# A two-layer attention and token-MLP kernel: weight loads in 256 KB pieces, and new order tables

## The chip, the cores and the metric

The kernel runs on one core of a Trainium2 chip. The metric is the time of one execution on the device in microseconds (us). The engines are TensorE (PE in the profile, with its weight loads as PEld), VectorE (DVE), ScalarE (ACT), GpSimd (POOL) and SyncE (SP), which here issues nearly all DMAs.

## The reference, cut to what matters

The input is x of 2048 tokens by 512 features, in bfloat16. Two blocks alternate, each twice, and both add their result to x.

```python
def _A_ref(x, wqkv, wo):                     # sliding-window attention, 32 heads of 16, window 256
    qkv = (x @ wqkv).reshape(B, S, 3, H, Dh) ...
    scores = einsum("bhqd,bhkd->bhqk", q, k) * Dh ** -0.5
    mask = (i - j >= 0) & (i - j < W)
    o = einsum("bhqk,bhkd->bhqd", softmax(where(mask, scores, -1e9)), v)
    return o... @ wo

def _B_ref(x, w1, b1, w2, b2):               # MLP over tokens
    u = gelu(einsum("bsd,sf->bdf", layernorm(x), w1) + b1)     # 2048 -> 1792
    return (einsum("bdf,fs->bds", u, w2) + b2).transpose(0, 2, 1)

x = x + _A_ref(layernorm(x), wqkv, wo);  x = x + _B_ref(layernorm(x), w1, b1, w2, b2)
x = x + _A_ref(layernorm(x), wqkv, wo);  x = x + _B_ref(layernorm(x), w1, b1, w2, b2)
```

## The kernel before

x stays on the chip as 16 tiles of 128 tokens (`x_sb`). A layer is one attention and one token MLP; there are two.

**Attention.** Queries go in four blocks (Q) of 512 tokens. For each block the normalised x is transposed into `xhT` (the first block by PE, L517, and copied out by DVE or ACT, L518; the others by DMA transposes issued from SP, L507), and `project` (L528) multiplies it by `wqkv`. K and Q are copied out of PSUM through a mask (`masked`, L544); V is copied (L599), transposed by DVE (L601) and spread into `v_sb` (L593). The heads form four groups t. For each block and group nine steps m follow: `emit_scores` (L689) writes two PSUM banks with quarter-array matmuls, ACT takes their exponential (`emit_exp`, L695), DVE or POOL multiply the edges of the window by a triangle (L713), and `emit_pv` (L739) multiplies by V into two other banks, 4 and 5. Two pairs of banks alternate for the scores, so the scores of step m + 2 wait for the exp of step m.

After the ninth step the two value banks are copied out, one into `oU` (L743) and one into `o2` (L744), by DVE or ACT, and only then may the next group write them. After every second group three small DMAs (`den_c`, L754) gather the softmax denominators and one of 256 KB (L755) moves half of `o2` into `oU`. `o2` has room for two groups, so a later copy into it waits for these DMAs. `job_inverse` and `job_normalise` then divide, and `job_outproj` (L656) multiplies by `wo` and adds to x, followed by the statistics of the next layernorm (`ln_stats`, bn_stats at L460).

**Token MLP.** `w1` has seven blocks fb of 256 columns, each in four quarters q of 512 tokens (256 KB). Blocks 0 to 2 have a home of their own, `w1buf`; block 3 takes over `xhT`, blocks 4 and 5 `k_sb`, block 6 `q_sb`, as soon as these are free (`w1_place`). `w1_half_dma` (L831) loads half a block of `w1buf`, 512 KB, `w1_dma` (L827) a quarter of the others. `u_product` (L862) and `job_u` make the products, `job_y` (L935) the second matrix with `w2` loads of 512 and 384 KB (`w2_dma`) into `w1buf` and `oU`. Parts of the first matrix product (`job_u_part`) and of the second are put between the attention's steps, so that PE has other work while ACT does exps.

**Order.** Every job makes operations (`Plan.op`) with the buffers they read and write, in a fixed numbering. Which engine does each one, and in what order each engine does its own, stands in the tables `ORDER`, written as two letters of `ALPHABET` per operation; `BANKS` gives the PSUM bank, 6 or 7, of each short-lived result. `arrange` reads them, and `needs` derives the semaphore waits. An engine goes through its own list strictly in order, SP with its DMAs included: what stands behind a waiting DMA issue waits too. SP's DMAs take 16 semaphores in turn, so that an issue also waits for the landing of the sixteenth before it.

**Beginning.** PE first does groups of ten small warm-up matmuls (L449), ten such groups in all, most of them before any result is needed. The loads come first on SP: x tiles 0, 1 and 2 to 3, the halves of the K and Q weights, x tiles 4 to 7, the V weights (into the home of w1's block 2, from where `turn_weights`, L437, reorders them). `first_half` (L564) makes the first K and Q group in two halves of 256 tokens each, so that the second half needs only the last two transposes.

Of the kernel before, what the change touches and what calls it, by code (L numbers as in the profile page):

```python
# [33 lines left out]
O0OmOsO6NqPBOzO5PFM0PKPAPSQYPZPEPfPJPPPVPjPtNkPNPYPyPeP4PcPiPsQAQHPoPxP3P-QRO3QGQVQKQbP7QoQfQkRXQvQUQaQeQ1Q-Q5QjQuRDORRKQ0Q4ROQsRUQ+RHRcQERhRNRTRbRmRg
RlRzR0RRSuR3R4R5SvSrSsS3S0S4SxSGS1S2SDS6S5SRSJSySVS7SNSwStSoSlSzSpSmSqTHSnTDTFTBTZS9S8S-TaThTNTVTOTiTRTSTWTdTeTLTJT0UFT5UGT1T6UAUBUqUUUvUZUjUfUrUdUbUk
VQU8UVUhUoUwVAVEVSVIWjWkVMVWVbYeVpVkYfVhVuV1VaX5X6VyV6VjVoV+VtV0V5WGWTWoV9WNWFWVWDW4WfWaWKXYXGWRWwWrXHWZW1WeW9WqWvW0XCZoW8XBXNXUXdXrYzXiXnZeYCXwXcX1Xh
XmXvX0X-YXYMYHaNZ3YTYaX+aOYuYGYLYQY1a+Y6YZY-Yta-ZEZIYyY5Y+ZDZPalZZZHZOZSZhboZrZlZMbpZyZgZ5cLZ+ZkZqZxaCbHaKZ1aVaHZ9aiaBaJaSaeaYayadarahbEaqaaaxa6a5bDbS
cObNbldZbMbhcPbybRb2babVb6cjcDbkbtb1cIb5aucbcCcHcgdrcocNcfcsa1c0clc4eVdAcrczdEbudRc3c-dDdQdVdUdcb9ehdmdbduc7dzdfeFd5eAcvdteHdyd4d-eMgIeQeDeYeueeeLeneP
eXeberd2ezfLe7emfDejeqfIeye6fCfQe2fVfHfPfUfcfjfrfnfvgrfmfzfqfyf3gff-f2gFe+gLf+gEgQiLgYgKgPgcgVh8gkgogTgbgwgjgngvg0fYhBgzhFf6hQhkhbhAhfiohEhmhMhKhqhxhU
h0h1h4heh-hjhNhpiDhwh3iIiaiQh+iCiXiHiNiehOiiibisixiWiTidihi3iriwi2i-ili+jGjKjHjRjYkZjVjUjbjojfi6jkjajejwkAj2jjj6jskEjvj1kLjtkPj5j-kWjDkIkejEkjkOkVkdko  # L40
kiknk1k2kSkTk5k6k7lwl8l5lzl2l9l6lIltlulFl3lxlXlPl0lLlTlylvl1l4lqlrlsl7mHmJmBmPmjmDmQmFlnmTmkmblomXmfmgmUmcmYl+lpl-mLmNmzm9m+mvnDnEm5m6mwnHnIm0nNnbnjnf
# [5 lines left out]
NzMYMXMvL5MmL6MHNRM8MzMnNhL7NVNWNbMIMTN3NiNjMUMoOPOMO-N9OgN-MVOZOoPnOrOCOwOxNrM1O9QZOBPWPXPRM2PbPOPhPdP6PpPqQJO4QLQMQXP8P9QdQCQDQTRYQpQqQrQhRAQ3QyOSRB
QtP+RIRJRZRCRoRpRaRsRqRSR6R7RxQFRvSASCSHSISFSESSSKSWSXSTSOSLSPSMSQSUSYSZSbSfSgTbTPTjTTTXTfUHT7UKT2T+T3UCT-ULUDT4UEUOUMUaUTUgUeUcUsU9UlU+UmUiUnUWUxUtVC
VFUyVGUXWlUuUzUYVNU0VLVYVOU2VeVVYgYjVmVnU4ViV3VxVrX7V4WmVzWAWUWpWJV8WEW5WnWXWMW6W7X8XaWPWYYkX9WcWQXIW3XLXbZpXMYlXWXPY0XEXtXXXlXFZfXpXyYDYYX3YnYBYsYqXq
YpZ4YPYEYSYVYRY3YxaPY4Y8Y9bAZBZKZUbBanZTZNbqZuZtbCZncMZ7ZvbrZ8aAaFaIaUaXaTaZatacbJa0bGaba8aQdacQbncRbUb0aRbsbccSbWckbXcTawcGavcVcddscicqbYcucncma2cXc6  # L50
# [10 lines left out]
AJAKASATAMAiALANBCAOAPBGCJCCB-CKAmApCLArAsCMCNCOCPBiAqB3BkB9BnBlBmCqClC0CmCrC5DGDACIDMC6DHCQDZDQDRCRCSDgFpCHDhDaDuDoAkD6FrEEEMCEFsCTFtENCBCUEcFuEdEwCV
ExErE6CWFQB+FXFLCXFeFYFMFRFfF6F7F-GEGAGKGFCYHpGVGfGrGnCZIFIGJOG-HEHAHIG0CDHXJQJTJRCFHtIUIBCGJSIKIPILIiIuCAI8JBJUI3I9JkJcKDKFKJKNCbKvKrKHLDLELIKGLNLUK4
LoL3MMMEMAMjNANGM7NPNHNZNpNfN7N8NvOIOVN+OAONCaOkODO2OvOEO8PHPDOyPUPIPMPvPlP0P1QmM3QxQ7RFQ8RMRQRWReRjR2RrRtSaScUNUPURTuUSU-VDVUVKU1U3VdTsU7VZU6VwU5TqVs
WITpWBWhWiWtWyWdWzWuYmXfW-XAXkXgXzTrX4YoYOYJXuYcYwYKYdYWTtZCZGZjaoZLapZRZbZ0aEZwaMakagbLbPa9bjbQb4b8cFbZcUcKcec2cWdGcYcacBdodwdYdecAeJeKeOeCepd+eaeget
# [6 lines left out]
BANKS = (
    "76766776777676767667766666677676777767776666667677677767666776666776676767677677667767766777666767676776776666677766676776776676677676676676"
    "766677666777777667666776777676766767776666776776766776677766")


class Res:
# [990 lines left out]
```

## Time and profile before

| | us |
|---|---|
| median of three runs (489.77 to 489.91) | 489.77 |
| the profiled execution, whole | 490.92 |
| its span, first to last instruction | 489.2 |
| PE busy | 480.0 (98%) |
| DVE busy | 335.3 (69%) |
| ACT busy | 319.7 (65%) |
| POOL busy | 199.6 (41%) |
| PE, PEld clock granted | 1.00 in every window |

The span contains everything from the first to the last instruction on any engine; the whole execution adds the start and end of the program. "Busy" counts time in which at least one instruction of the engine ran, so PE can be busy and yet lose a little where a group starts late behind another that still drains. L numbers are lines of the kernel. In a row of the timeline the text in brackets is the idle time of the engine before that instruction and what ended it. The first attention lies between 12 and 161 us of the span, its MLP up to about 235, the second attention up to 395, and the last MLP to the end.

### The profile page before, as it was taken

Reading aid. Unit: us, or ns where it says so; the run is one execution under the profiler, and the core shown is the slowest. Engines: PE = TensorE matmul, PEld = TensorE weight load, DVE = VectorE, ACT = ScalarE, POOL = GpSimd, SP = SyncE. Lnnn points to the kernel's source line nnn. Section 1 sums busy time; section 2 is a strip of 40 time slices with the busy share of each in tenths; the row PEclk is TensorE's granted clock in tenths of the full one; section 3 lists DMA queues with packets and bytes.
Section 4 is the critical chain, followed back from the end, with each engine's and each line's share of the span. In section 5 each row is a group of like instructions: output and inputs, shape, how many; then the busy total and the mean of one; then the engine's idle time right before and its main releaser. Section 6 shows DMA issues by size and latency. Waiting matters only on the chain.

```text
span 489.2 us, 17263 instructions
## 1 busy us (share of the span) xinstructions
PE 480.0 (98%) x7706; PEld 255.4 (52%) x7706; DVE 335.3 (69%) x707; ACT 319.7 (65%) x391; POOL 199.6 (41%) x365
## 2 busy tenths in 40 slices
PE   7999998999999999999999999999999999999997
PEld 6544555555556444444445555556556544444444
DVE  7999998889988550246798777999977646122123
ACT  4999998999989313302767889999999940240000
POOL 5988884534726100022624544465644721000000
PEclk9999999999999999999999999999999999999999
DMA  6442024400228780350024300130222957030842
GB/s 194 92 119 56 27 60 100 70 5 27 27 58 223 215 228 1 107 147 5 1 44 132 89 27 3 37 62 6 68 70 77 261 148 204 0 98 10 228 150 86
DMA packets 83722, 43.59 MB, mean 89 GB/s; under 512 B 19008, under 2 KB 82624, under 8 KB 83648
## 3 DMA queue, kind: packets, MB, share of 16 engines
q1 hardware_dynamic: 79776, 42.48, 32.1%
q0 software_dynamic: 3872, 0.02, 1.2%
q8 instruction: 60, 0.98, 0.8%
q14 instruction: 14, 0.11, 0.1%
HBM read 32.51 MB, written 2.10 MB: 71 GB/s over the span
## 4 chain that ended last, share of the span: by engine, by line
PE 91%; ACT 5%; DMA 1%; DVE 1%; SPq 1%; issue 0%
PE ps L859 20%; PE ps L932 19%; PE ps L526 17%; PE ps L684 14%; PE ps L733 12%; PE ps L653 6%; ACT p_sb L695 4%; PE ps L777 1%; DMA x_sb<-in_A_x_dram 1%; PE ps L919 1%; SPq L352 1%; PE ps L446 0%; DVE o L358 0%; DVE q_sb L537 0%; ACT vT L360 0%
## 5 line engine op out<-in xcount | busy, mean ns | idle before, releaser
L695 ACT ACTIVATE p_sb<-ps 128x1024 bf16<-128x1024 f32 (+8 forms) x288 | 261.1, 974 | 23.5 <-PE ps L684 18.5
L712 POOL TENSOR_TENSOR p_sb<-p_sb,edge 128x256 bf16<-128x256 bf16 (+2 forms) x223 | 106.8, 494 | 102.7 <-ACT p_sb L695 88.0
L684 PE MATMUL ps<-q_sb,k_sb 64*64 64x288 bf16 (+8 forms) x2816 | 107.2, 250 | 1.4 <-ACT p_sb L695 1.1
L526 PE MATMUL ps<-xhT,wqkv 128*128 128x512 bf16 x376 | 95.6, 382 | 0.2 <-DVE q_sb L537 0.2
L733 PE MATMUL ps<-p_sb,v_all 64*64 64x288 bf16 (+8 forms) x2816 | 89.7, 246 | 1.6 <-DVE o L358 1.1
L684 PEld LDWEIGHTS ps<-q_sb,k_sb 64*64 64x64 bf16 x2816 | 53.6, 106 | 53.4 <-ACT p_sb L695 32.9
L733 PEld LDWEIGHTS ps<-p_sb,v_all 64*64 64x64 bf16 x2816 | 58.4, 107 | 14.8 <-issue 5.5
L932 PE MATMUL ps<-uT,w1buf 128*128 128x512 bf16 x280 | 64.3, 380 | 0.0
L936 DVE SCALAR_TENSOR_TENSOR x_sb<-ps,b2col,x_sb 128x512 bf16<-128x512 f32 x31 | 22.6, 745 | 51.0 <-PE ps L932 50.9
L712 DVE TENSOR_TENSOR p_sb<-p_sb,edge 128x256 bf16<-128x256 bf16 (+2 forms) x177 | 45.3, 275 | 14.1 <-ACT p_sb L695 12.7
L526 PEld LDWEIGHTS ps<-xhT,wqkv 128*128 128x128 bf16 x376 | 30.6, 98 | 39.7 <-issue 5.4
L482 POOL TENSOR_TENSOR rstd<-vare,mhalf 128x4 f32<-128x4 f32 x15 | 15.2, 1015 | 86.3 <-DVE vare L480 48.6
L859 PE MATMUL ps<-xh_sb,w1buf 128*128 128x512 bf16 x192 | 46.3, 381 | 0.0
L460 DVE BATCH_NORM_STATS2 stats<-x_sb 128x6 f32<-128x512 bf16 x64 | 42.9, 681 | 1.8 <-DMA x_sb<-in_A_x_dram 1.6
L932 PEld LDWEIGHTS ps<-uT,w1buf 128*128 128x128 bf16 x280 | 26.3, 98 | 32.3 <-issue 1.3
L537 DVE TENSOR_TENSOR k_sb<-ps,half 128x1024 bf16<-128x1024 f32 (+1 forms) x29 | 34.7, 1197 | 5.0 <-PE ps L526 4.9
L492 ACT ACTIVATE xh_sb<-x_sb,shift,rstd 128x512 bf16<-128x512 bf16 x8 | 6.4, 810 | 48.1 <-POOL shift L486 48.1
L537 DVE TENSOR_TENSOR q_sb<-ps,even 128x1024 bf16<-128x1024 f32 x29 | 35.3, 1217 | 1.9 <-PE ps L526 1.5
L932 PE MATMUL ps<-uT,oU 128*128 128x512 bf16 x154 | 35.5, 380 | 0.0
L653 PE MATMUL ps<-wo_sb,oT 128*128 128x512 bf16 x128 | 32.4, 381 | 0.0
L859 PE MATMUL ps<-xh_sb,k_sb 128*128 128x512 bf16 x128 | 30.8, 380 | 0.0
L586 POOL TENSOR_TENSOR v_all<-vB,v_all 128x512 bf16<-128x512 bf16 (+1 forms) x16 | 23.5, 1474 | 16.8 <-DVE vB L601 16.6
(89 smaller groups left out, 453.1 us busy)
## 6 DMA issues: line engine op xcount, KB each, us to landing
w1buf<-in_B_w_dram SPq DMA_DIRECT2D x20, 512.0 KB
oU<-o SPq DMA_DIRECT2D x16, 256.0 KB
k_sb<-in_B_w_dram SPq DMA_DIRECT2D x16, 256.0 KB
w1buf<-in_B_w_dram SPq DMA_DIRECT2D x10, 384.0 KB
oU<-in_B_w_dram SPq DMA_DIRECT2D x6, 512.0 KB
oU<-in_B_w_dram SPq DMA_DIRECT2D x6, 384.0 KB
q_sb<-in_B_w_dram SPq DMA_DIRECT2D x8, 256.0 KB
xhT<-in_B_w_dram SPq DMA_DIRECT2D x8, 256.0 KB
```

What stands on the lines that cost most here:

```text
L460: dve(lambda e: e.bn_stats(stats[:, t, :], x_sb[:, t, :]), 690, prio, reads=[R("x", t)], writes=[R("stats", t)])
L526: last = e.matmul(ps[:, b, :], lhsT=wqkv[:, c, c0:c0 + P], rhs=xhT[:, buf, c, :], start=(c == 0), stop=(c == 3))
L537: return e.tensor_tensor(dst, src.unsqueeze(2).to_broadcast([P, n, 2, w]), mask[:].unsqueeze(1).unsqueeze(3).to_broadcast([P, n, 2, w]), o ...
L586: return e.tensor_tensor(d, src.unsqueeze(2).to_broadcast([P, k, 2, DH]), v_all[:, 0:32].rearrange("p (h d) -> p h d", h=2).unsqueeze(1).t ...
L653: last = e.matmul(ps[:, b, :], lhsT=oT[:, buf, t, i * P:(i + 1) * P], rhs=wo_sb[:, t, :], start=(t == 0), stop=(t == 3))
L684: last = e.matmul(ps[64 * c:64 * c + 64, 2 * half + r, 32 * i0:32 * i1], lhsT=k_sb[rows, ring, t, kb % 16, :], rhs=q_sb[rows, t, c, 32 * i ...
L695: latest[0] = plan.op({ACT: (170 + int(2 * (512 - c0) * 0.84), lambda e: e.activation(p_sb[:, slot, :, c0:512], ps[:, 2 * half:2 * half + ...
L712: return e.tensor_tensor(v, v, g, op=ALU.mult)
L733: last = e.matmul(ps[64 * r:64 * r + 64, B_O + (c ^ r), 32 * i0:32 * i1], lhsT=v_all[rows, col:col + 64], rhs=p_sb[rows, slot, r, 32 * i0: ...
L859: r = e.matmul(ps[:, b, :], lhsT=blk[:, n, (ft % 2) * P:(ft % 2 + 1) * P], rhs=xh_sb[:, 4 * g + n, :], start=(first and g == quarters[0] a ...
L932: r = e.matmul(ps[:, b, :], lhsT=blk[:, fc, (st % 2) * P:(st % 2 + 1) * P], rhs=uT[:, fc, :], start=(fc == 0), stop=(fc == NFT - 1))
L936: dve(lambda e: e.scalar_tensor_tensor(x_sb[:, st, :], ps[:, b, :], b2col[:, st:st + 1], x_sb[:, st, :], op0=ALU.add, op1=ALU.add), 750, prio,
```

## The change

The half-block load becomes two quarter loads, everywhere it is used (twenty loads of 256 KB in place of ten of 512 KB), and the bookkeeping of `w1buf` goes by quarters. The V weights and the w2 blocks, which lie in the same memory, now name the quarters that they cover.

```diff
-        load(w_nat, w_src[:, :, 2 * D:3 * D], 1 << 19, -100, writes=[R("w1", 2, 0)])
+        load(w_nat, w_src[:, :, 2 * D:3 * D], 1 << 19, -100, writes=[R("w1", 2, 0), R("w1", 2, 1)])
...
-                    reads=[R("w1", 2, 0)], writes=[R("wqkv", 2, t, r)], prio=-96)
+                    reads=[R("w1", 2, 0), R("w1", 2, 1)], writes=[R("wqkv", 2, t, r)], prio=-96)
...
             if fb < 3:
-                return w1buf[:, fb, 4 * q:4 * q + 4, :], [R("w1", fb, q // 2)]
+                return w1buf[:, fb, 4 * q:4 * q + 4, :], [R("w1", fb, q)]
...
         def w1_half_dma(fb, h, prio):
-            load(w1buf[:, fb, 8 * h:8 * h + 8, :], w1v[:, 8 * h:8 * h + 8, fb * 256:(fb + 1) * 256], 1 << 19, prio, after=latest,
-                 writes=[R("w1", fb, h)])
+            for q in (2 * h, 2 * h + 1):
+                load(w1buf[:, fb, 4 * q:4 * q + 4, :], w1v[:, 4 * q:4 * q + 4, fb * 256:(fb + 1) * 256], 1 << 18, prio, after=latest,
+                     writes=[R("w1", fb, q)])
...
-                return flat[:, 0:NFT * 256].rearrange("p (f s) -> p f s", f=NFT), [[R("w1", k, h)] for h in range(2)]
+                return flat[:, 0:NFT * 256].rearrange("p (f s) -> p f s", f=NFT), [[R("w1", k, 2 * h), R("w1", k, 2 * h + 1)] for h in range(2)]
```

All five order tables and the table of banks are replaced. The first line of SP's, as an example (two letters are one DMA):

```diff
     "sync": """
-AAABACADAGAEAIAHCiAFCwDjCsDIDSCtC7DWDqHKGgGhEXEWG6EYEZGaGbGZGcKlEnK+IYIaKkIbHRLOIZKTKfKdKeKgMZMcMbMaOcObOaOdP2TxQPQNQQPwPrQOOWIvQiQzQnRfTnRyR8R+R9OlRk
...
+ABAAACAIAEADAGAHAFCiCwCsDjCtDSDIC7G8GiEWHMEZDWEXEYGjEnEoDqGdGcGbGeIcIbLTIdHTHUIeKqLDKpKjKiKkKlMfMhMgMiKXKYOhOiOgOjQTQUQtQoQVQWP2P8RDPxR4OcRlQ5SDSCSERM
...
```

Read as operations, SP's first nine DMAs were x 0, x 1, x 2 to 3, K half 1, Q half 2, Q half 1, x 4 to 7, V weights, x 8 to 9; they become x 1, x 0, x 2 to 3, x 4 to 7, Q half 1, K half 1, Q half 2, V weights, K half 2. Among the first operations of DVE, five that build `edge` stand ahead of the statistics where two did, and of the four tiles of the first block tile 0 is normalised first, then 1, 3 and 2. One of PE's warm-up groups moves ahead of the first scores, and the projection of Q's second group behind them.

In all, PE has the same 916 operations, DVE 716 in place of 707, ACT 373 in place of 375, POOL 354 in place of 361, and SP 204 DMAs in place of 194. Where copies out of PSUM, edge multiplications and layernorm applications are done changes between DVE, ACT and POOL, and so do their places throughout.

More of the change, by code (lines that the diff above doesn't have):

```diff
@@ L34 @@
[L34 to L41, printed above, removed]
@@ L47 @@
[L47 to L50, printed above, removed]
@@ L61 @@
[L61 to L64, printed above, removed]
@@ new lines @@
+NYLsLWL0LaNRL7LlMDLiLrMILzL6MQMCL3MVMHMPMjNHMrMnMUMcMvN2MzMmM3L+M-MqMyNENmNKM2M+NTNWNdNDNjMYNtNJNQNaNzNgN7NiN-OUNsOMNyN6OQPEOZN+OLOkOPOWOdOoOtOvOnOsOz
+PsO6OyPANwO5PHO-PLQeM6PYPGPKPQPPPbPlPVPfPTPzPePkPpPoNqP+P4PiPyQGP3P9PuQNQFQMQXO9QQQbQhRdQuQlQqOXQaQ1QgQkQpQ7RFQ-Q0RJQBRQQ6Q+RERUQKRaRNRiRXRnRTRZRhRmRs
+RrR5R6QyS0R9R+R-S3S6S7S9SxS1TASMS+S4SJTBS2SXSPSySTSbS8S5SrSsS-TCStTLTTTNTUSzTHTjTJTXTDTfTbSuTcTYTkTgTnToSvSwTFTPTRT6T7T-UGUHUAULUMU1UwUxUpUlUjUqUfUhU2
+UuUnUaVCVWVOVYVnVGUbWpVcVhWqVKVvVqYkV4YlV0V7VgVpVSX-WAVuWEVzV6V-WMWuYAWDWbWTWZWJWLWlWQWgW+XeXMWXW2WxZuXNW7WfWkXDWwY5XIXaW1ZkXjW6XCXHXTXoYIXxXtX2XiXnYd
@@ new lines @@
+X7YFXsaTYNX1X6YSZ9YZYEYMYRYgaUY0YWY7bEZAYfYzY4ZFY-ZKarZOZEZJZVbFZNZfZUZYZnbuZrZxZSbvZ4Z-ZmcRZqaEZwZ3aIbNZ7aQabaNaDaoaHaPaYakaea4ajaxanbKagawbAa3a-bJbY
+cUbTbrbScVbXbnbgb8dfb4bqbzcJcpcAbbb7cOb-a0chcIcNcmdxcucTcya7clc6crc+ecdGcxc5dKb0dXc9dFdbcDdidJdWdseod0dad6c1eAdhdleHeMeOdzd5d-eTdBeXeGeKefe1eleSeugRd9
+eWeye6eeeifTfDetfLeqfQexe5fCfYe9fdfKfPfXfcfkfrfvfzg0f3f7gofuf-fyf6gHfGgOf+gGgUiVgZgNghiGglgTgYgegtgcgxg5fgg9gkgsgwhKhuhOg4g8hJhahNhWhehlgCiyhphwhUh0h+
+h7hohtiCh-iJhzh6iNhXiSiBiIiaikihiMiRiXioilisi2hYi7iginirjBidi1jJi6jAjIjRivjbjQjUjfjijlkjjejpjkjukKjyj6jojtkAjEkEj5j-kDkOkJkSkVj2kckZkgj3kdkoktjNkYkykf
@@ new lines @@
+knkskxlAk-jOlDlElFmAmGl3l9l6mBl4lSmCl5lPmHmDlZlVl7mElhmFldl8l+l-l0l1l2mImPmNmdmemlmhmRmTmZmimLmpmamqmmmtlxlymulzmJmXmVm9nNnHnDnRnOnSnEm+nIm5m6nbnXnpnc
+nlnhnYn1nmntninqn2nxn5nynun6oAn9""",
+    "vector": """
+AcAdAeAfAgAWAUAVAaAYA7A5A8AQA6BBA-A9BDBAA+BFBEBKBIBHBdBOARBfAXBWBZBbAhDUBgAbAZBqBrBcCgBaBeBhBsBjCrChCdFjBoC0BnC1FlAsBmDGFhBvDlBwFnFiDcDgFoBzDoDCFmFkDu
+DzFpFrB0JJB7EAB8D0JNFbEHGTEUEVEsENJKEIEgEhE1E-ExGlFAF4JPFVFMFYFNJLFGFHF1HpFIGBHqGQGGHrHcJMIGGaGZHOIHGzIIG+G0JOJQG1HGJTIUHLHWHXHeIVHjHnHfI5JRH3H-HzHyIA
@@ new lines @@
+INIXIOKsIoIaIZItIpIlKaI6JuJFJbH5JBJVJcIqI8JHJ6JlJkH6JiJ7K2KEKAKFJvLwH7J8JwKGKVLhKIKgLVLxKLMMKNKMLILFK7K8LRLZLfNZLcLbNSLjLkMFL9MKL4L5MTLyNIMeMdMsN3MXN4
+MxL-MAMNM1NnM5NGN5NoNXNpMZNcNbNhMOMtNlOVMBMuOCODPFOTObOeOfOuOFOmOqOxMaPtNxPCO2O1QfO3M7POPaPcPWPXPnPdPUP1PjP7M8PvPwM9O+QRQIQJQdReQPQvQSRfOYQ4RGQ9QnRHQw
+QCRPROQDQxRYQERgRIRwRuRpQzRyR8SBSASGQLSISNSOR3SKSLSYSQSZSUSRScSdSeSVSSSaSWShSfSkSmTVTdTlThTpTZT8UBUEUIT9UNUQUJT+UFUKURUUUSUXUZUmUkUgUiUyUrUsU3UoUzVXUt
+U0VoVQUcVEUdVFUeVHU4WrU5VjVIVkU8U6VLVAVBVJVbVMYmVNVyVTU+VeYpVsVtV9VUWvWCYBWaWdYCYDWVVVWWWRXAWSXBWsWPWtXgYqXOWoXRY6XFZlXLXhXUXSXcYrXyXdXzYtYxYeX9XwX5YH
@@ new lines @@
+YPYQYUZ+YYYbY2YXaVY3YjY+YKZCZDZMasYLaWatbGavauZZZTbwZpZ0bHZ1cSaCaKaLZ2ZzaGaOaSaaaZafbPaXa6aqazahaibCbabMbxbybIcWbibhbRdgb+cqcXbda2becYa1cZdyckcoa8cbcs
+ctcgcfb1edcEdddecFb2duepdndmc2eNdCeDe2c3eEeReJe3c4ead+ekejfUdDeserfNfVfFe-dEe+fma9f0fbflb3g1g2gpf1f2gqa+fHdQf9fIiWdOfJiHgrg3gfgghBgdgjdVdTfhg7gvhAhMhv
+hDhIfihHhfhcizhRhVh3hyhniAfjh9h5iUgEiPijiZimiYiQiuhZifiejDi+iwjLjWixjdjVjMjhkkjrjzj8kLj9jFj0kMklkNkGj1kmgFjGjHk2kHj4k4kbkik0k1kvlCk9kelGjPlMk8lOlTlUlR
+lQlalblWlXlcliljlelflYlklglnlllrlqlpmfmjmbmnmrmvm-nJnPm7nTnFndnZnnn3njnrnznvn7oBn+""",
+    "scalar": """
@@ new lines @@
+AlAjAiBMBQBUBSBYAmAnCfB2CpCkCvC4CzD2C+DFBuDLDPDYDfDnByDdDyDtB6D+D5GvEDELEGEQEbEkErEwEfE5E+E0FDFLFQFXFeFUFzF6F-GEGLGPGWGgGoGsGyG5HAHFHJHRHZHiHmHvH2H+ID
+IMIRIgIkA4IsIwI2I-JEJaJfJnJrJzJ3J-KDKQKUKdKnKvKhKzK5LALHLMLQLYLeLnNPLtL1L8MEMJMRMWMkMoMwM0M4NANFNLNUNeNkNuN0N8OAONOROaOlOpOwO0O7PBPIPMPZPRPmPgP0PqNrP5
+P-QHQOQYQcQiQmQrQ2Q8RARKRRRVRbRjRoRtR7R2SHR1SlTMTKTITETOTWTeTqTiTaTmTGSnTQTSUvVDVPVZVdViVwVrV5V8U-V1WBWNWFWcWUWKW-WmWhXfW3WyZvW8XEXJXbXkXpXVXuX3YJX8X0
+YGYOYTYaYhY1Y8ZBZGZLZPZWZgZaZoZsZyZ5aAaFaJbOacaRapala5aybLbBbZbQbUbsbob9b5cKcBbccPcicncvczc7c-dHdLdYdcdjdtd1d7eBeIePeUeYegemevgSeze7fEfMfRfZfefsfwf4f8
@@ new lines @@
+gAgIgPgVgagigmgugyg6g+hLhPhbhghmgDhqT1hxh1h8iDh4iKiOiTibiiipiti3i8jCjKjSjcjgjmjjjqjvj7kBkFkPkWkTkUkakhkpkukzlBlHltk6lNmOmQmSmgmUmomcmkmMmsmKmwmYmW""",
+    "gpsimd": """
+AJAMAKANASALATAOAPBCBGCEB+CJCDCHCKAoCLArCCCBCMCNApCOB3CqClAqBiB4BkCmBlC5AtC-DHDADMC6CPAkDZDaCQDhDQDRDpCRFqFsD-DvFtFvCSEED6D7FwCTERCUEMElEcESEmFuEdEtCV
+CWE6EyE7FEE2FRFZFfFSF0FgGACXCYF7GFF8GXB9GMGhGRCZHsGtGpHBG6B-HCHKG2HSHaIJCIHwJSJUJWIEISIWJYIhCAJXIxCGJACFI3JgJoJsJ0J4I7KRKeKoKHKJKwKWK6K0KKLBLNLJLSK9L2
+LoLuMGMSMpCaMlNBNCNfNVNMNNN1NvOBN9OOOSOEOGOIOKOHPDO8PJOJPNO4PSPhMbPrP6CbQAQZQjQsQ3RBRCRLRWRSRcRkRvRxRzR0SgSiSjUTUVTvUWUYVaTxT0TzVRVxU7U9VfV2V3V+TyWGWO
@@ L70 @@
 }
 BANKS = (
[L72 to L73 removed]
+    "76676666677777767667766677767676676777766766677677667767776667766766677776777667676766677676677766767676766667676766676776776676676677676676"
+    "766667776776766777666667676776766767776677777666676767677677")
 class Res:
```

26 lines of the change are left out of this document (7 added, 19 removed).

## The prediction

> **What bounds the kernel now.** I read the page first: busy times, then the 40 slices. The whole program is one TensorE (PE) stream; DVE and ACT are nearly as full for the first 60 us.
>
> ```profile
> PE 480.0 (98%) x7706; PEld 255.4 (52%) x7706; DVE 335.3 (69%) x707; ACT 319.7 (65%) x391; POOL 199.6 (41%) x365
> PE   7999998999999999999999999999999999999997
> DVE  7999998889988550246798777999977646122123
> ACT  4999998999989313302767889999999940240000
> ```
>
> Then the table of windows (us, then busy PE, PEld, DVE, ACT, POOL, clock, DMA share, GB/s), two stretches of it:
>
> ```profile
> 36.70:48.90 12.20, 12.01 (x244) 6.07 (x241) 12.16 (x27) 12.07 (x20) 10.70 (x28) 1.00 0.28 56
> 73.40:85.60 12.20, 10.94 (x245) 6.12 (x236) 10.61 (x23) 10.34 (x12) 5.20 (x8) 1.00 0.49 100
> ```
>
> The clock is full in every window, so time is lost only where PE waits: 489.2 - 480.0 = 9.2 us without a matmul, 2.65 of them after the last one. Last I read the timeline at the two places that lose most. The beginning (start, length, engine, line, operation, idle before it and its releaser):
>
> ```profile
> 7.45 1.57 DVE L476 TENSOR_SCALAR xh_sb<-x_sb,agg,rstd 128x512 bf16<-128x512 bf16 x2
> 8.94 0.41 DVE L358 COPY xhT<-ps 128x512 bf16<-128x512 bf16 x1
> ...
> 10.25 0.69 DVE L460 BATCH_NORM_STATS2 stats<-x_sb 128x6 f32<-128x512 bf16 x1 [0.91 <-DMA x_sb<-in_A_x_dram]
> 10.86 0.41 DVE L358 COPY xhT<-ps 128x512 bf16<-128x512 bf16 x1
> ```
>
> DVE stands idle 0.91 us until x tiles 4 to 7 land, because a bn_stats of them is queued ahead of the copy (10.86) that PE needs; PE's second half projections start only at 11.32, after 0.65 us without a matmul. And the longest wait in the attention:
>
> ```profile
> 79.28 0.69 SPq L352 DMA_DIRECT2D den_c<-o  x1
> ...
> 82.18 0.69 DVE L358 COPY o<-ps 128x512 f32<-128x512 f32 x1 [1.56 <-PE ps L526]
> ...
> 82.92 0.41 PE L733 MATMUL ps<-p_sb,v_all 64*64 64x288 bf16 x8 [1.10 <-DVE o L358]
> ```
>
> The copy of a finished attention bank into o2 may start only when the DMAs that read the previous o2 have landed. One of these (8 KB) left SP last, at 79.28, behind transposes that hold SP up to 3.04 us each and a 512 KB weight load. PE lost 1.17 us over its usual step.
>
> **The change part by part.** PE's work is the same: both orders hold 916 groups with 270 changes between quarter-array ("cells") and full matmuls. Such a change costs 0.14 us into cells and 0.09 out of them (0.357 against 0.219 for a score group, 0.955 against 0.863 for a projection), so equal counts mean equal time: 0. Summing each PE group's excess over the shortest of its own kind and predecessor, before loses about 12.4 us in excesses over 0.06: 2.7 up to 12 us, 7.6 in the first attention, 2.1 in the second. Only these can move.
>
> *The beginning.* x tiles 4 to 7 move from seventh to fourth place in SP's queue. From the first bn_stats (2.87, 128 KB landed) to the one at 10.25 (1,792 KB) the queue delivers 1,664 KB in 7.38 us, 225 KB/us. So they land at 6.9 instead of 10.25; the first Q weights (1,280 KB) at 8.0, K (1,536 KB) at 9.1, the second Q (1,792 KB) at 10.3; the V weights keep their bytes ahead (11.6). DVE now does five small edge operations first (bn_stats at 3.1 instead of 2.87), then normalises tile 0 by 6.7 and tiles 3 and 2 at 8.4 and 8.9. That last takes 0.42 like the others; in before it took 1.15 beside POOL's memset of spread (L974, 7.92 to 8.87), and if the memory work POOL now does there slows it as much, it ends at 9.6. Last transpose plus 0.25: first projection at 9.1 (9.9) against 9.64. The bn_stats ahead of the second copy no longer waits, so the four half projections (4 x 0.437) run through and end at 10.9 (11.7) against 12.39: 1.5 (0.7) us sooner. K's first weights land as they are needed; 0.5 us later would cost as much.
>
> The Trainium skill (GPSIMD Engine Reference, Key points) says that GpSimd shares its SBUF interfaces with VectorE and contends with its two-port modes; the row of 1.57 us for two normalisations agrees, and by that rule the 0.7 is the likelier gain. Here POOL's casts beside the copy at 8.94 left it at 0.41.
>
> Does it last? ACT has no idle time worth naming from 12 to 73 us, so PE can't outrun it. ACT's masks of the half projections begin about 0.7 sooner and its 0.93 us gap ahead of the second goes: 1.6. Up to the end of the scores of head group 1 in the second query block ACT's queue differs by one more fill of ones (1.04, early, in idle time), one weight turn more (0.30) and one V copy less (0.61): -0.3. So ACT can follow. I take -1.1; ends -0.4 and -1.7.
>
> *The o2 wait at 82.9.* In the new queue, behind the DVE copy come: den_c 0.69, den_c 0.58, a transpose (1.2 to 3.0), den_c 0.69, two weight pieces 2 x 0.59, the o2 to oU move 0.59: 4.9 to 6.7 us, plus 1.9 from issue to landing as before (76.57 to 79.09, less its issue). Its data also follow the two pieces (512 KB at 265 GB/s, the rate of the fullest window, 2.0 us): landing 7 to 9 us after the copy. The copy is wanted again about 8.3 us after (9.8 us of PE work between the banks' ends, less 1.5). Wait 0 to 0.7, so -0.9 of the 1.17; ends -1.2 and, if transposes hold SP for 3 us and the pieces are as late, +1.0.
>
> *Bank copies.* Each end of nine value products needs two copies of 0.683 us before the next group may write. With both on DVE that takes 1.52 with handoffs. Counting the PE work the order puts between: before has 7 gaps of 1.55 to 1.56 with both on DVE, which lost 0.60 together (0.086 each), and one of 0.95, short by 0.57, which lost 1.29. After has 12 such gaps and three short ones (1.16, 1.33, 1.33: 0.74). 5 x 0.086 = +0.4; 0.74 x 1.29/0.57 = 1.68, +0.4. Together +0.8; ends 0 and +3.6 (below).
>
> *Waits of scores for exp.* Counted through both orders, 22 groups before and 23 after have less PE work behind the group they depend on than the chain between them lasts (mostly one exp, 1.03 us, and handoffs): 0, ends -0.7 and +0.7. ACT has two instructions fewer, DVE nine more, POOL seven fewer.
>
> *The pieces.* Ten more issues of 0.59 us on SP, which waits more than 350 us altogether: 0. PE's largest excesses name no such load, so finer pieces free nothing directly. Without cover each would push what stands behind it in SP's queue by 0.59. The Trainium skill (DMA: Bandwidth & Descriptors, Measured) asks for transfers of 1 MiB or more for 75% of the peak, which speaks against pieces; here windows of 256 and 512 KB loads run at 265 GB/s and a 0.97 share, so I add nothing for size.
>
> *A moved load.* Ahead of the second quarter of the fourth weight block, wanted where the first MLP begins (about 176 us), SP now issues the 896 KB of a later w2 block. From the first of that burst 4,250 KB have 19.1 us of PE work; at 265 GB/s (259 KB/us) they take 16.4 and 2 to land. 0; end +2.4 at the 223 GB/s (218 KB/us) of the window from 146.8 to 159 us, where loads were not always queued.
>
> Sum: -1.1 - 0.9 + 0.8 = -1.2. Against the profiled span: 489.2 - 1.2 = 488.0. That execution took 490.92 in all, 1.15 over the median of the runs, 489.77; the difference carried to the median gives **488.6 us**. What a measurement can tell from no change is 0.2%, 0.98 us.
>
> **The rivals.** *The gain is swallowed (0.20).* For: ACT is at 12.07 of 12.20, and one more Q mask (1.40) stands early in its queue, so by the end of the first nine exps it is only 0.3 sooner. Against: that mask is given back by 66 us. If the 0.3 is all that stays, and the o2 wait merely moves: 489.5.
>
> *Copies queue behind DVE: slower (0.12).* Place: the 15 tight or short gaps. For: DVE is 12.16 of 12.20 busy at 37 to 49 us and gets nine more operations. Price: the worst tight gaps lost 0.19 and 0.24, so 12 x 0.22 = 2.6; the short one lost 0.72 more than it lacked, so 0.74 + 3 x 0.72 = 2.9; 5.5 against 1.9 is +3.6, with -1.1 and -0.9 +1.6: 491.4. It decides once a gap loses more than 0.26 on average (1.9 + 2.0 over 15). Against: most tight gaps in before lost only 0.03 or 0.04.
>
> *The weight burst comes late (0.06).* At 223 GB/s PE waits 2.4 us at the first MLP: 488.6 + 2.4 = 491.0. Against: that window's share of 0.81 left engines idle.
>
> *The change does what it says, as costed: 0.62.*
>
> **How the numbers follow.** The forecast lies only 0.2 beyond the bound, so of its 0.62 I count 0.50 as faster and 0.12 as same; same 0.32 with the swallowed gain; slower 0.18 from the copies and the late burst. Range: the best ends of the beginning, of o2 and of the score waits (-1.7 - 1.2 - 0.7) with the copies' +0.8 give -2.8, 487.0; above, 491.0 takes in the late burst and leaves out the copies' case (0.12): 486.9 to 491.0.
>
> **What would show it.** Right: bn_stats of tiles 4 to 7 without a DMA wait; PE's last half projection by 10.9 to 11.7; exps of the first query block 0.3 to 0.8 sooner, about 1 us at 66; no wait over 0.7 at the third bank copy of the second block. Wrong: PE waits on wqkv's DMA before 12 us; PE L733 waiting on DVE copies for more than 4 us in all; PE L859 waiting on a DMA near 176; a gain at 12 us that is gone at 66.

## The result, and the profile after

The changed kernel took 490.85 us (median of 16 runs, 489.96 to 491.66), the kernel before beside it on the same chip 489.75 (16 runs, 488.82 to 490.15): a ratio of 1.0021, 95% interval 1.0014 to 1.0029. It is 0.2% slower, clear of the noise; 488.6 and faster was forecast. The time lies in the range, at its upper end, but the change went the other way.

The page of the changed kernel, busy times and slices:

```profile
PE 480.5 (98%) x7706; PEld 256.3 (52%) x7706; DVE 338.2 (69%) x716; ACT 319.1 (65%) x391; POOL 193.8 (40%) x358
PE   8998999999999999999999999999999999999997
DVE  7999999989996451256887777999987646120313
ACT  6998999999999123303568789999999940240000
```

The two gains are there to be seen: the first slice of PE goes from 7 to 8, the seventh (73 to 85 us) is full. The windows say the same, with one exception (us; then busy PE, PEld, DVE, ACT, POOL, clock, DMA share, GB/s):

```profile
36.70:48.90 12.20, 10.88 (x202) 5.49 (x204) 11.99 (x26) 10.28 (x16) 10.65 (x23) 1.00 0.58 141
73.40:85.60 12.20, 12.20 (x282) 6.80 (x281) 11.70 (x22) 11.84 (x14) 7.61 (x12) 1.00 0.56 112
```

Between 73 and 86 PE is busy for 12.20 us where it was 10.94: no wait for o2. But between 37 and 49 it is busy for 10.88 where it was 12.01, and ACT, which was full, stands idle for 1.9 us. The timeline shows why (start, length, engine, line, operation, in brackets the idle time before and its releaser):

```profile
39.48 0.63 SPq L352 DMA_DIRECT2D oU<-o  x1
40.15 0.58 SPq L352 DMA_DIRECT2D wo_sb<-in_A_wo_dram  x1
40.78 1.41 SPq L352 DMA_DIRECT2D den_c<-o  x2
42.23 1.22 SPq L507 DMA_TRANSPOSE xhT<-xh_sb  x1
...
46.52 1.04 PE L526 MATMUL ps<-xhT,wqkv 128*128 128x512 bf16 x4 [1.21 <-DMA xhT<-xh_sb]
```

The last of the four DMA transposes for the third query block leaves SP only at 42.23, behind a weight load of 256 KB that isn't wanted before the first output projection (68.99 in this trace), and two den_c. PE waits for it at 46.5. A second wait stands at the beginning of the first MLP:

```profile
167.81 2.90 SPq L352 DMA_DIRECT2D oU<-in_B_w_dram  x2
170.75 1.17 SPq L352 DMA_DIRECT2D xhT<-in_B_w_dram  x1
...
177.20 1.89 PE L860 MATMUL ps<-xh_sb,xhT 128*128 128x512 bf16 x8 [0.61 <-DMA xhT<-in_B_w_dram]
```

That is the moved load: the second quarter of w1's block 3, issued behind 896 KB of w2, lands after PE wants it. In the kernel before, the last of the four transposes left at 40.11, and PE had no wait at either place:

```profile
40.11 1.19 SPq L507 DMA_TRANSPOSE xhT<-xh_sb  x1
...
45.34 1.04 PE L526 MATMUL ps<-xhT,wqkv 128*128 128x512 bf16 x4
...
178.60 1.89 PE L859 MATMUL ps<-xh_sb,xhT 128*128 128x512 bf16 x8
```

The beginning, last, went as forecast:

```profile
7.83 0.73 DVE L476 TENSOR_SCALAR xh_sb<-x_sb,agg,rstd 128x512 bf16<-128x512 bf16 x2
8.48 0.69 DVE L460 BATCH_NORM_STATS2 stats<-x_sb 128x6 f32<-128x512 bf16 x1
9.27 0.42 DVE L358 COPY xhT<-ps 128x512 bf16<-128x512 bf16 x1
...
9.07 2.12 PE L562 MATMUL ps<-xhT,wqkv 128*128 128x256 bf16 x16
```

The bn_stats of tiles 4 to 7 has no wait before it, and the four half projections run from 9.07 to 11.19 in one piece; before, the second half began at 11.32.

One puzzle was left. The profiled executions of the two kernels have nearly the same span (489.2 before, 488.9 after), yet the medians differ by 1.1 us. Either the profiled execution of the kernel before was a bad one, or that of the changed kernel a good one. The numbers speak for the first: its 490.92 us lie above all 16 runs of the kernel before (highest 490.15), while the 490.65 of the changed kernel lie near its median.

### The profile page after: what moved, and what is told of

Same layout as the page of the kernel before. It is cut to its first block, busy times and chain, and to the rows that moved or that the text cites. A ratio compares the mean times of both kernels' runs of the same rounds, so it can differ in the third digit from the quotient of the medians.

```text
span 488.9 us, 17259 instructions
## 1 busy us (share of the span) xinstructions
PE 480.5 (98%) x7706; PEld 256.3 (52%) x7706; DVE 338.2 (69%) x716; ACT 319.1 (65%) x391; POOL 193.8 (40%) x358
## 3 DMA queue, kind: packets, MB, share of 16 engines
q1 hardware_dynamic: 79936, 42.48, 31.4%
## 4 chain that ended last, share of the span: by engine, by line
PE 82%; ACT 5%; POOL 4%; DVE 4%; DMA 2%; SPq 2%; issue 1%; POOLq 0%
PE ps L933 19%; PE ps L860 17%; PE ps L526 14%; PE ps L684 12%; PE ps L733 10%; PE ps L653 5%; ACT p_sb L695 5%; SPq L352 2%; PE ps L446 2%; POOL p_sb L712 1%; DMA xhT<-in_B_w_dram 1%; POOL xh_sb L489 1%; PE ps L777 1%; DMA xhT<-xh_sb 1%; DVE k_sb L537 1%
## 5 line engine op out<-in xcount | busy, mean ns | idle before, releaser
L695 ACT ACTIVATE p_sb<-ps 128x1024 bf16<-128x1024 f32 (+7 forms) x288 | 261.3, 974 | 23.6 <-PE ps L684 19.7
L712 POOL TENSOR_TENSOR p_sb<-p_sb,edge 128x256 bf16<-128x256 bf16 (+2 forms) x227 | 110.5, 500 | 128.1 <-ACT p_sb L695 109.1
L712 DVE TENSOR_TENSOR p_sb<-p_sb,edge 128x128 bf16<-128x128 bf16 (+2 forms) x173 | 45.2, 279 | 15.4 <-ACT p_sb L695 11.7
L537 DVE TENSOR_TENSOR k_sb<-ps,half 128x1024 bf16<-128x1024 f32 (+1 forms) x28 | 33.4, 1194 | 5.6 <-PE ps L526 5.3
L537 DVE TENSOR_TENSOR q_sb<-ps,even 128x1024 bf16<-128x1024 f32 x26 | 31.6, 1217 | 2.9 <-PE ps L526 2.7
L908 ACT ACTIVATE uT<-ps,b1col 128x512 bf16<-128x512 f32 x16 | 10.4, 680 | 30.9 <-PE ps L860 30.9
L905 DVE TENSOR_TENSOR v_all<-v_all,ps 128x512 f32<-128x512 f32 x12 | 8.1, 687 | 29.3 <-PE ps L860 29.3
```

What stands on the lines that cost most here:

```text
L537: return e.tensor_tensor(dst, src.unsqueeze(2).to_broadcast([P, n, 2, w]), mask[:].unsqueeze(1).unsqueeze(3).to_broadcast([P, n, 2, w]), o ...
L695: latest[0] = plan.op({ACT: (170 + int(2 * (512 - c0) * 0.84), lambda e: e.activation(p_sb[:, slot, :, c0:512], ps[:, 2 * half:2 * half + ...
L712: return e.tensor_tensor(v, v, g, op=ALU.mult)
```

## The experiments

All ratios are to the kernel before, run beside them on the same chip. The four groups below ran on four different chips, and the medians of the kernel before differed between these: 490.51 (runs 1 to 4), 491.17 (5 to 8), 490.84 (9 to 12), 490.51 (13 to 15), with runs from 488.7 to 494.5. So kernels of one group are compared with each other, and others by their traces.

To add up where PE loses, each PE group's step (from the end of the one before it to its own end) is compared with the usual step of its kind behind the same kind, the 20th percentile over all traces. What is above that is called its excess. The sums stand in the table of the next section.

### 1. The kernel before, unchanged

> The kernel before, unchanged. Theory: the 1.17 us that PE lost at 82.9 us in its profile, waiting for the copy into o2, was an accident of that one execution (it took 490.92 us in all, its median is 489.75), so there were no 0.9 us for the change to win. A new profile then has a span near 488.0, no idle time over 0.4 us ahead of the value product (L733) near 82, and the median is 489.7. Rival: the wait is the kernel's own and the execution differed elsewhere; then the wait of about 1.1 us is there again, whatever the span.

Median 490.18 (12 runs), ratio 1.0002 [0.9982, 1.0023]; the profiled execution took 489.5, span 487.8. Its timeline at the place of the old wait:

```profile
80.45 0.69 DVE L358 COPY o<-ps 128x512 f32<-128x512 f32 x1 [0.57 <-PE ps L526]
...
81.20 0.41 PE L733 MATMUL ps<-p_sb,v_all 64*64 64x288 bf16 x8
```

The DVE copy into o2 waits 0.57 us and not 1.56, and the row of the value product names no idle time before it. The brackets name PE both times, but it is the same den_c: its last part landed 0.08 us before the copy in the first trace (at 82.10) and 0.07 before it here (at 80.38). So theory and rival are both half right. The wait for this den_c is the kernel's own, but what it costs PE differs from execution to execution. In four traces that have the old order at this place PE lost 1.17 us (before), 0.19 (run 1), 0.65 (run 7) and under 0.05 (run 8).

### 2 to 4. The transpose early, the quarter ahead, and both

In SP's list (Q2 i1 is the transpose of token tile 1 of the third query block):

```diff
   Q2 i2, Q2 i0,
+  Q2 i1,
   den_c, Q2 i3, o2 -> oU, wo, den_c, den_c,
-  Q2 i1,
   w1 piece, w1 piece, wo, ...
```

```diff
   ... w1 block 4 q 3,
+  w1 block 3 q 1,
   w2 512 KB, w2 384 KB,
-  w1 block 3 q 1,
   w1 block 0 q 2, ...
```

> The changed kernel with one DMA moved in SP's queue: the transpose of token tile 1 of the third query block stands right behind the transpose of tile 0, ahead of the first den_c, where in the changed kernel it follows the 256 KB move into oU, a 256 KB load of wo and two den_c. Theory: the 1.21 us that PE waits at 46.5 us for this transpose is a large part of the loss; it goes, and 1.0 to 1.3 us of it stay at the end: 489.7 (1.1 less than the changed kernel's 490.85). Rival: ACT is full there, PE only waits for exps instead, or den_c comes later and the copy into o2 with it: 490.5 or more.

> The changed kernel with the second quarter of w1's block 3 issued ahead of the 896 KB of w2 instead of behind them. Theory: the 0.61 to 0.77 us that PE waits for it at 177 us go, nothing else moves, as ACT and DVE have idle time there: 490.1 (0.7 less). Rival: the whole burst is bound by the DMA engines' rate and the next load in it is late instead, near 180 to 210 us: 490.8, no change.

> Both moves in the changed kernel. Theory: the two losses lie in different stages and add: 1.8 to 2.0 us less than the changed kernel, 488.9 to 489.1, which is 0.6 to 0.9 us under the kernel before. Rival: as in the single runs, 490.2 to 490.8.

| | median | ratio |
|---|---|---|
| 2, transpose early | 493.00 | 1.0043 [1.0027, 1.0059] |
| 3, quarter ahead | 489.63 | 0.9977 [0.9961, 0.9992] |
| 4, both | 491.37 | 1.0012 [0.9996, 1.0027] |

The quarter did what was expected: no excess near 177 in its trace, and it is faster than the kernel before. Run 4 against run 2 prices it at 1.63 us. The transpose moved early made it worse, by 1.74 us (run 4 against run 3), as the rival had it. The timeline of run 2:

```profile
39.87 1.19 SPq L507 DMA_TRANSPOSE xhT<-xh_sb  x1
41.10 0.74 SPq L352 DMA_DIRECT2D den_c<-oU  x1
...
47.49 0.69 DVE L358 COPY o<-ps 128x512 f32<-128x512 f32 x1 [2.51 <-DMA oU<-o]
...
48.60 0.41 PE L733 MATMUL ps<-p_sb,v_all 64*64 64x288 bf16 x8 [2.05 <-DVE p_sb L712]
```

and its windows (columns as above):

```profile
46.00:49.00 3.00, 0.95 (x22) 0.41 (x20) 1.51 (x5) 1.32 (x3) 0.54 (x2) 1.00 0.74 219
49.00:52.00 3.00, 2.54 (x63) 1.95 (x56) 2.97 (x8) 1.77 (x3) 2.86 (x9) 0.63 0.30 92
52.00:56.00 4.00, 3.67 (x75) 1.81 (x68) 2.94 (x8) 3.34 (x5) 2.94 (x7) 0.85 0.02 4
```

The moved transpose could not start before 39.87, because POOL normalises that tile only by then: SP stood waiting in front of it from 36.5. The den_c behind it left at 41.10 in place of 37.37, the move out of o2 came later too, DVE's next copy into o2 waited 2.51 us for it with the edge multiplications queued behind, and PE waited for these. Then PE's clock fell: its mean is 0.63 over the next 3 us and 0.85 over the four behind them. That is the mechanism of the o2 wait, now in the first query block: a transpose brought forward for its own sake had held up what stands behind it.

### 5 to 8. The changed kernel again, edges sooner, and one part of the change at a time

Run 5 is the changed kernel. Run 6 has the quarter ahead of w2 and on POOL:

```diff
+  edge Q0 t0 m5 (186)  ahead of those of m6 and m8
+  edge Q0 t1 m0 (208, 209)  ahead of that of m2
+  edge Q0 t1 m6 (250, 251)  ahead of a constant and of that of m8
+  edge Q0 t2 m2 (285)  ahead of that of m3 and of the normalisation of Q2 i1
```

Run 7 is the kernel before with each `w1_half_dma` of 512 KB replaced by its two halves in the same place. Run 8 is the kernel before with the changed beginning: on each engine what the changed kernel has done by 12.0 us first, then all else in the old order.

> The changed kernel, unchanged, beside the others on one chip. Theory: it loses against the kernel before by what its own trace shows late: the second quarter of w1's block 3 (0.6 to 1.5 us at 177 to 181) in every execution, while the 1.21 us for the DMA transpose at 46.5 came from one DMA queue that was 1.8 us late that time and come in some executions only. A new profile has the wait near 177 again and perhaps not the one near 46; ratio to the kernel before 1.001 to 1.003. Rival: the transpose's wait is the kernel's own and is there again.

> The changed kernel with the quarter ahead of w2 (as in the third run), and on POOL four edge multiplications moved ahead of work that is not wanted so soon: those of step 5 of head group 0 and of steps 0, 6 of group 1 and 2 of group 2, all in the first query block. Theory: POOL's late edges gave back most of what the new beginning gains; PE's waits for them (0.36, 0.27, 0.67 and 0.46 us in the third run's trace) go, and 1.0 to 1.6 us of them stay: ratio to the third kernel 0.997 to 0.998, some 488.3 where that one is at 489.6. Rival: ACT is full there, PE then waits for the exps instead, and no more than 0.3 us stay: ratio 0.9995 to 1.0.

> The kernel before with the pieces alone: its own order, each load of 512 KB replaced in its place by its two halves. Theory: the pieces cost nothing, as SP has idle time: ratio 1.000, within 0.0015. Rival: ten more issues of 0.5 to 0.6 us on SP come ahead of den_c, the moves into oU and the transposes, and cost 0.5 to 1.2 us: ratio 1.001 to 1.0025.

> The kernel before with the changed kernel's beginning alone: on each engine the operations that the changed kernel has done by 12.0 us come first, in its order (15 of PE, 32 of DVE, 7 of ACT, 17 of POOL, 9 DMAs), and then all others in the order before. Theory: the second half projections end 1.1 to 1.6 us sooner, and 0.8 to 1.3 us of it last to the end, as ACT's queue is not longer: ratio 0.997 to 0.9985. Rival: the gain is swallowed in the first attention, because ACT and POOL are full: ratio 0.9995 to 1.0005.

| | median | ratio |
|---|---|---|
| 5, changed kernel | 491.28 | 0.9991 [0.9971, 1.0012] |
| 6, edges sooner, quarter ahead | 489.57 | 0.9966 [0.9946, 0.9987] |
| 7, pieces alone | 490.84 | 0.9993 [0.9970, 1.0016] |
| 8, beginning alone | 491.83 | 1.0009 [0.9986, 1.0033] |

Run 5: the wait near 177 was there again, 1.53 us, and so was the one near 46, 1.60, as the rival said. In runs 5 and 6, as in the first trace, one of the transpose's 16 parts landed 1.8 to 1.9 us after the other fifteen; in run 3, where this part of SP's order is the same, all landed within 0.2 us and PE did not wait. So the place in SP's queue alone does not make the wait; it needs the late part too, which came in three of these four traces.

Run 6 is 1.7 us below run 5, but its edges brought little: the waits named went from 1.76 us to new ones of 0.31, 0.40 and 0.34 (the last for an exp). Run 7 can't be told from the kernel before: the pieces alone are neither gain nor loss that could be seen. Run 8 neither: up to 12.2 us its excess is 0.79 against 2.10 in run 1, and from there to 61 us it is 4.18 against 2.73. Set in front of the old order, the new beginning is given back at once in this trace; the medians are too uncertain to tell.

### 9 to 12. The transpose where its data are ready, and den_c first in the kernel before

The transpose now stands three places ahead of its own in the changed order, and three behind that of run 2:

```diff
   Q2 i2, Q2 i0, den_c, Q2 i3, o2 -> oU,
+  Q2 i1,
   wo, den_c, den_c,
-  Q2 i1,
```

Run 10 adds the quarter ahead of w2, run 11 also the four edges. Run 12 is the kernel before with one move on SP, in the second query block:

```diff
   den_c, den_c,
+  den_c,
   Q3 i0, o2 -> oU, w1 half 512 KB, Q3 i3,
-  den_c,
```

> The changed kernel with the transpose of token tile 1 of the third query block two places less far ahead than in the second run: behind the move into oU and ahead of the 256 KB load of wo and the two den_c. There its data are ready (POOL normalises that tile by 39.3 to 39.9, and the move leaves SP at 39.8), so SP isn't held. Theory: it is issued near 40.0 instead of 41.9 to 42.2, out of reach of the instruction fetch of 16 KB that runs at 43.7 to 44.2 in all four traces and made one of its sixteen parts 1.8 to 2.0 us late in three; all parts land within 0.4 us, PE's wait of 1.2 to 1.6 us at 47 goes, and the wait for the quarter of w1 near 177 stays: 1.0 to 1.4 us less than the changed kernel, which lay at 0.9991 of the kernel before on the last chip and at 1.0021 on the first; ratio 0.9965 to 0.9995. Rival: the transposes are slow as such and the next one pays: no change against those ratios.

> As the ninth, and the second quarter of w1's block 3 ahead of the 896 KB of w2. Theory: the loss at 177 us (0.77 to 1.53 us in three traces of the changed kernel) is its own and adds: 0.8 to 1.5 us less than the ninth, and no wait over 0.2 us near 177. Rival: the next load of the burst is late instead: less than 0.3 us.

> As the tenth, and the four edge multiplications of the sixth run sooner on POOL. Theory after the sixth run's trace, where three new waits of 0.31 to 0.40 took the place of four of 0.27 to 0.67: 0.3 to 0.7 us less than the tenth, near 487.5 where the kernel before has 489.75. Rival: nothing is left, as ACT sets the pace there: 0 to 0.2 us.

> The kernel before with one den_c (the one that left SP last at 79.28) moved ahead of a transpose, the move into oU, a 512 KB load and another transpose, to the place right behind the two other den_c. Theory: the wait for the copy into o2 near 82 us (1.17 us in the first trace, none in the second) then can't come in any execution; where it did it also lowered PE's clock, so the runs spread less, and the median is 0.3 to 1.0 us lower. Rival: the wait is rare, and the kernel's spread is from elsewhere: ratio 0.9995 to 1.0005 and as wide a spread.

| | median | ratio |
|---|---|---|
| 9, transpose ahead of wo | 490.44 | 0.9992 [0.9977, 1.0007] |
| 10, and the quarter ahead | 488.64 | 0.9953 [0.9937, 0.9970] |
| 11, and the edges | 488.95 | 0.9966 [0.9952, 0.9980] |
| 12, kernel before, den_c first | 489.39 | 0.9976 [0.9963, 0.9989] |

The timeline of run 10 at both places:

```profile
39.20 0.63 SPq L352 DMA_DIRECT2D oU<-o  x1
39.87 1.29 SPq L507 DMA_TRANSPOSE xhT<-xh_sb  x1
...
45.05 0.81 PE L526 MATMUL ps<-xhT,wqkv 128*128 128x512 bf16 x3 [0.16 <-issue]
...
174.90 1.89 PE L860 MATMUL ps<-xh_sb,xhT 128*128 128x512 bf16 x8
```

The transpose is issued at 39.87, its parts land at 42.27 to 42.38, and PE has no wait for it; the same in run 9 (42.36 to 42.48). At 174.90 the first group that reads the moved quarter follows without idle time. Run 9 still has its 1.58 us there, and run 10 is 1.80 below it. The changed kernel itself did not run on this chip, so the transpose alone has no price from medians. The edges brought nothing: their rival held. Run 12 is 1.45 us faster than the kernel before by the move of a single DMA of 8 KB. Its runs spread nearly as widely, though (3.1 us against 3.4), so the spread isn't from this wait alone. That the wait also lowers PE's clock, as was expected, isn't shown: behind the 1.17 us of the first trace the clock stays at 1.00.

### 13 to 15. All on one chip

> The changed kernel, unchanged, on the same chip as the next two. Theory: it has both its own losses, the transpose near 47 us and the quarter of w1 near 177, and lies at 0.999 to 1.002 of the kernel before, whose own time differs from chip to chip by the waits for o2. Rival: without them in its trace it is as fast as the next one.

> The tenth kernel again: the changed kernel with the transpose ahead of wo and the quarter of w1 ahead of w2. Theory: the sum of the two waits, 2.0 to 3.1 us in three traces of the changed kernel, comes back in full: 1.8 to 2.8 us less than the thirteenth, and faster than the kernel before again (0.994 to 0.997). Rival: only one of them counts, the rest is given back later: under 1.3 us.

> The tenth kernel with the beginning of the kernel before: the operations that the kernel before has done by 12.5 us come first on each engine, in its order, then all others in the changed order. Theory after the eighth run (the new beginning in the old order brought nothing: 1.3 us less lost up to 12 us, 1.9 more from 12 to 49): the gain is swallowed by the first attention, where ACT, DVE and POOL are full, and this kernel is at most 0.4 us slower than the fourteenth. Rival, as the prediction had it: the 1.1 us last, and it is 0.8 to 1.3 us slower.

| | median | ratio |
|---|---|---|
| 13, changed kernel | 490.96 | 1.0004 [0.9988, 1.0020] |
| 14, as run 10 | 488.51 | 0.9958 [0.9944, 0.9973] |
| 15, as run 10 with the old beginning | 490.53 | 1.0003 [0.9985, 1.0021] |

Run 14 is 2.45 below run 13, whose trace has 1.26 us at the transpose and 1.72 at the quarter: nearly all of both comes back. The theory of run 15 fell: with the old beginning the kernel is 2.0 us slower, more than even the rival said. Its trace loses 2.65 us up to 12.2 where run 14 loses 1.12, and the rest further on:

```profile
11.27 1.05 PE L562 MATMUL ps<-xhT,wqkv 128*128 128x256 bf16 x8 [0.61 <-DVE xhT L358]
...
14.42 0.62 PE L684 MATMUL ps<-q_sb,k_sb 64*64 64x288 bf16 x16 [0.68 <-DVE k_sb L537]
```

So the new beginning is worth 2.0 us in front of the order that was made with it, and nothing that could be seen in front of the other (run 8).

## Why the prediction was wrong

Three of its steps failed. The moved load was set at 0 and cost 0.8 to 1.7 us in the traces; a transpose in the first query block, which the sum did not have, cost 1.3 to 1.6; and the 1.1 us won at the beginning were gone by 66 us.

Excess of PE's groups in us, by what they wait for, in two traces of the kernel before, three of the changed one and one of the version with both moves:

| | forecast | before | run 1 | after | run 5 | run 13 | run 14 |
|---|---|---|---|---|---|---|---|
| beginning, up to 12.2 | -1.1 | 2.70 | 2.10 | 1.49 | 1.07 | 1.21 | 1.12 |
| first value product of a group (bank copies, o2) | -0.1 | 2.40 | 1.30 | 1.37 | 1.24 | 1.38 | 1.40 |
| scores (exps) | 0 | 5.62 | 6.04 | 4.84 | 4.83 | 4.85 | 4.42 |
| other value products (edges) | not in the sum | 0.58 | 0.56 | 1.58 | 1.46 | 1.65 | 2.18 |
| transpose near 47 | not in the sum | 0.04 | 0.04 | 1.28 | 1.60 | 1.26 | 0.00 |
| quarter near 177 | 0 | 0.01 | 0.01 | 0.77 | 1.53 | 1.72 | 0.00 |
| all others | 0 | 1.94 | 1.80 | 1.71 | 1.86 | 1.83 | 1.72 |
| sum | -1.2 | 13.29 | 11.85 | 13.04 | 13.60 | 13.90 | 10.84 |

*The beginning: right up to 12 us, but it does not last.* -1.1 forecast; the means of two and three traces give 1.26 - 2.40 = -1.1. Its first marks (no DMA wait, half projections done by 11.19) came as named; the slower case, 11.7, was not put to the test, as POOL's memset came only at 9.54, behind the normalisations (0.73 us for two). For 66 us the prediction named about 1 us sooner as right and a gain gone by then as wrong, and the second came. The first exp ends at 13.5 to 14.0 us in three traces of the changed kernel, at 15.68 and 15.08 in two of the kernel before; the 27th at 40.6 to 41.2 against 41.06 and 40.32, still ahead of the late transpose; the 54th, the last of head group 1 in the second query block, at 66.5 to 66.8 against 65.98 and 65.24. Without the late transpose (run 14) it is 65.31. This is the swallowed gain, which had 0.20, in the stretch it named. Only the reason seems to be another than the Q mask on ACT: the edges (below), as the table has it; no run shows that by itself. Run 15 shows what the new beginning is worth to the new order, not that it lasts against the kernel before.

*The o2 wait: the mechanism right, its size wrong.* The prediction took -0.9 from one trace, though it noted that this execution lay 1.15 us over the median and carried that difference along as if it came from elsewhere. It came, most likely, from this wait: in run 1 it cost PE 0.19 us, and by this trace the row of the first value products hardly moves (1.30 to 1.24-1.38). In the measurement of the result, where the kernel before ran at 489.75, little can have been left to win. In others there was more: run 12 gained 1.45 us by this one den_c. This is also the likely reason why the change did not come out alike everywhere: the changed kernel ran at 490.85, 491.28 and 490.96 in three measurements, the kernel before at 489.75, 491.17 and 490.51 beside it. This stays an inference: no run looked at the wait for o2 beside the result again.

*The bank copies: too dear.* +0.8 forecast. Without the o2 wait the row is 1.23 and 1.11 before and 1.24 to 1.38 after, so the tight and short gaps more cost some 0.2. Their rival (491.4, not far from the time measured) isn't the cause.

*Exps and edges: 0 forecast, and 0 in sum, by two errors; that they cancel is luck.* The scores lose 1.0 us less and the value products, waiting for edges on POOL, 1.0 more, nearly all of it before 61 us. The prediction named ACT's queue and didn't look at where POOL's edges stand. Doing them sooner (runs 6 and 11) only brought the waits back elsewhere: between 12 and 61 us ACT, DVE and POOL are all nearly full.

*The moved load: mis-sized, and it decided.* The step costed it at 0 with 0.7 us of slack left (16.4 + 2 of 19.1), and gave its late end 0.06. It was late by 0.77, 1.53 and 1.72 us. The term that was too small is the 16.4 us for the bytes. They went by 265 GB/s, the rate of a window in which loads were queued throughout, and here they were not (columns as above):

```profile
157.40:162.00 4.60, 4.60 (x47) 2.19 (x46) 2.61 (x7) 1.71 (x2) 2.26 (x4) 1.00 0.74 214
162.00:164.00 2.00, 2.00 (x11) 0.88 (x10) 0.48 (x1) 0.00 (x0) 0.00 (x0) 1.00 0.25 72
164.00:171.00 7.00, 7.00 (x92) 3.33 (x90) 4.10 (x8) 1.01 (x2) 0.00 (x0) 1.00 0.98 289
```

The first load of the burst leaves SP at 157.40, but between 159.4 and 162.8 SP issues only three den_c, and the DMA engines run nearly empty. 4,256 KB had moved by 175.32, 17.9 us after 157.40, or 243 GB/s; in runs 5 and 13 it took 18.2 and 18.6. The last part of the quarter landed 1.7 to 2.2 us later (at 177.07 in the first trace), close to the 2 assumed. So the load came 19.7 to 20.7 us after the start of the burst and not 18.4, and PE's work left it 19.1. That is the late burst, which had 0.06, at a price of 0.8 to 1.7 us where it had 2.4. Run 10 against 9 and run 4 against 2 price it: 1.80 and 1.63.

*The step that was missing: SP's queue in the first query block.* The prediction wrote of the pieces that without cover each issue would push what stands behind it, set 0, and walked the queue only behind the o2 copy of the second block. In the first block the new order puts a weight load and two den_c ahead of a transpose whose data come late. There one part of it landed late in all three traces of the changed kernel ("What the hardware showed"), and PE lost 1.26 to 1.60 us; in run 3, at the same place but without a late part, PE lost nothing. Three entries earlier the parts landed together and PE did not wait (runs 9, 10 and 14). No rival named it. What it is worth in the median is known only together with the quarter: 2.45 us (run 14 against 13).

With what the traces of run 1 and of the changed kernel show, the sum is: beginning -0.8, o2 and copies 0, exps -1.2, edges +1.0, transpose +1.3, quarter +1.3, others 0: +1.7 (a mean of 13.5 against 11.85), against +1.1 measured. Against the mean of both traces of the kernel before, 12.57, it is +0.9. The rest can't be told from so few traces: the three sums of the changed kernel differ by 0.9, the two before by 1.4.

The forecast itself was there to be had: with two DMAs elsewhere in SP's list the changed kernel is 2.0 to 2.2 us faster than the kernel before (runs 14 and 10).

## What to carry to other kernels

Compare the profiled execution with the median before a wait in it is counted as a gain: if it lies above, the largest wait may be what made it so, and a second profile of the same kernel settles it. When an order table is replaced, walk the whole DMA queue, and for each transfer on the path write down when its data are ready, when it is issued, and when it is wanted. A DMA may be too late (behind loads that have time) and too early (it holds the queue until its data are ready), and here the right place was three entries away from either. And a rate read where loads are queued throughout does not hold for a stretch in which the issuing engine waits.

## What the hardware showed

*Beside an instruction fetch a single part of a transfer can come late.* The third part of the changed kernel's page, by queue (packets, MB, share of 16 engines):

```profile
q8 instruction: 60, 0.98, 0.8%
```

These are packets of 16 KB, one every 4 to 10 us in the first attention, about 1 us each. In the changed kernel one starts at 44.1, while the transpose issued at 42.23 lands: 15 of its parts arrive by 44.70, the last at 46.47. Over the 17 traces of this study, 404 transposes could be followed in all 16 parts. One part came more than 1.2 us after the middle one in 36 of them. In 35 of these a fetch had begun between 0.6 us before and 0.3 after that middle landing; among the transposes without a fetch in this interval it was 1 of 322, with one 35 of 82. That the fetch holds one DMA engine is an inference from this; which engine carries what wasn't to be seen. The Trainium skill (Runtime: NRT & Kernel Launch, Instruction fetch mechanics) says that a sequencer fetches instructions in blocks of 16 KiB through a DMA queue of its own, at a cost that is mostly hidden. The size agrees; the cost was not hidden where PE waited for the transfer beside it.

*Behind a pause of 2 us PE's clock was halved for 3.41 us.* In run 2 PE was idle for 2.05 us in one piece and busy for 0.95 of 3 us; the clock in its trace is then 0.5 from 49.78 to 53.19, which gives the means of 0.63 and 0.85 above. Run 4, with 0.60 of 3 us busy, has the same 3.41 us at 0.5. After the idle pieces of 1.42 and 1.56 us in run 13 the windows still show 1.00. So in runs 2 and 4 the stall cost more than its own length. Such a stretch also comes without a moved transpose: 9 of the 70 runs of the kernel before beside runs 1 to 8 have a mean clock of 0.996 or 0.997, as 3.41 us at half the clock in some 489 us give; none of the changed kernel's 40 has. Which wait it is there, no trace shows. The Trainium skill (TensorE: Matmul & The Clock Gate, Part 1) names an idle window of about 3.4 us for this. Here a shorter pause was enough.
